# A second backward pass that lives in the first one's buffers: deferred w2 gradients, weight transposes in steps, one fixed order on the Sync queue

## The chip, the core and the metric

The kernel runs on one core of a Trainium2 chip. The core has a matmul engine (TensorE, PE in the profile, with its weight loads listed as PEld), VectorE (DVE), ScalarE (ACT), GpSimd (POOL), and SyncE (SP), whose only work here is to issue transfers. SP, ACT and POOL each keep a queue of the transfers that they issue (SPq, ACTq, POOLq in the profile); all of these are carried out by the core's 16 DMA engines. Each engine works through its own instruction list in order and waits at semaphores for the others.

The metric is the device time of one execution, in microseconds. Before the change the median of three runs is 2060.66 us (2057.24 to 2063.25).

## The reference: what is computed

A block with two branches and its whole gradient. L = 2048 positions, D = 576 channels, F = 4608 hidden units, N = 128 states; all inputs and outputs are bf16.

```python
xn = _layernorm(x)
s  = _A_ref(xn, ...)              # state-space convolution: y = conv(xn, K) + xn * Dskip
g  = _silu(_B_ref(xn, w1, w3, w2))   # gated FFN: (silu(xn @ w1) * (xn @ w3)) @ w2
out = x + s * g
# the convolution's kernel, per channel d and lag l
K = einsum("dn,dnl,dn->dl", Cc, exp(dt * A * l), dt * Bc).real
# and then the vector-Jacobian product for x and 11 parameters
_out, _vjp = jax.vjp(_f, A_u, A_A_re, ..., B_w1, B_w3, B_w2)
return (_out, *_vjp(grad_out))
```

So the kernel returns the output (out_0), the gradient of x (out_1), of the convolution's parameters (out_2 to out_9), and of w1, w3 and w2 (out_10, out_11, out_12). The change touches only the backward half.

## The kernel before, in words

The work is written in a tile language. A planner turns it into one instruction list for each engine: it places every instruction when its inputs and its buffer are ready in the planner's own reckoning of time, and among ready ones it takes the one with the earliest due time. `self.at(us)` sets the due time for what follows (L99). A tile pool has a number of buffers for each tag; a new tile waits until the oldest one of its tag has been used for the last time. A pool that is opened where another one was closed shares that memory, and its tiles wait for the users of the old ones.

The forward half and the first half of the backward (up to about 850 us) are not touched. The rest, in `backward` (L1080), has four parts:

- *The convolution's backward* (`ssm_bwd_conv`), in four quarters, beside the first groups below. It writes gK_dram and GXN_dram (the part of the gradient of the normalised x that comes from the convolution).
- *The groups* (`phase6_load` L1139, `phase6_group` L1171). F is cut into 18 groups of 256. For each, G and U are read back from HBM; ScalarE and VectorE turn them into the hidden h (tile h_n) and two factors (gg_n, gu_n). Then `ph` matmuls (L1188) multiply the output's gradient, kept transposed in goT and goTt, with w2's rows transposed (w2T); VectorE multiplies the result into gg_n and gu_n, which now are the gradients of the gate and the up branch. Three more steps follow: they are stored to GG_dram and GU_dram from the Sync queue (L1200); `phase6_grad2` (L1204) forms w2's gradient from h_n and go_o (two blocks of 32 matmuls in a group, L1215); `phase6_grad13` (L1222) forms those of w1 and w3 from xn and gg_n, gu_n (L1233, L1240, L1242). ScalarE copies each result out of PSUM into a tile gw, and GpSimd issues its store.
- *The parameter chunks* (`param_quarter`, L957), 36 of them. Each reads qT (a transposing transfer on the Sync queue, L969 through L1137), gK (two transfers on the Sync queue into a tile gz that was zeroed by GpSimd, L864 and L966) and pz (ScalarE's queue), makes 16 matmuls (L977), and keeps VectorE for 16 instructions (L986, L988, L991) that sum into S_all. After the last one `phase5_final` (L994) turns S_all into out_2 to out_8; its input loads (L82) and its buffers come after the chunks' ones.
- *The input-gradient tiles* (`phase6_inputs`, L1250), 16 of them, 128 positions each. A tile reads its rows of GG_dram and GU_dram transposed (ggc, guc; two transposing transfers on the Sync queue) and multiplies them with w1 and w3 transposed, 36 blocks of 128 hidden units each (tiles wTB_w in the profile): 144 matmuls into px (L1277). VectorE adds the convolution's part (L1280), and `ln_bwd_tile` (L1284) takes it back through the layernorm and stores out_1, in turn from the Sync and the ScalarE queue. ggc and guc have two buffers each.

w1 and w3 are transposed in two parts: blocks 0 to 11 by ten transposing transfers in one run during the groups (five for each weight, one for each 128 rows), into a pool of their own, and blocks 12 to 35 by ten more, in a pool that is opened after the groups' pools are closed, together with the pool of ggc and guc and with go_o, goT and goTt given up:

```python
                    self.nat_transpose(ggc[:], self.GG_dram[i])
                    self.nat_transpose(guc[:], self.GU_dram[i])
                    if i == 0:
                        wT = wT + [self.load_wT(wB, FA, FT)]
```

The due times in `backward(700, 36, 90, 15, 18, ...)` say: groups from 700 us on, 36 us each; chunks from 1060 us on, 15 us each; tiles from 1348 us on, 18 us each. Nothing else fixes the order in which chunks, stores and tile transfers stand on the Sync queue.

## Time and profile before

| | |
|---|---|
| median of the runs | 2060.66 us (2057.24 to 2063.25) |
| the profiled execution: its time, its span | 2069.67 us, 2067.9 us |
| mean granted PE clock | 0.952 |
| busy: PE, PEld, DVE, ACT, POOL | 1792.2, 1310.5, 1390.4, 880.4, 333.3 us |
| transfers over the span | 411.29 MB, 199 GB/s |
| px matmuls (L1277) | 2 x 1152 |
| w2-gradient matmuls (L1215) | 1152, in 36 blocks |
| w1/w3-gradient matmuls (L1233) | 2 x 1152 |
| stores of gw on POOLq | 144 of 64 KB, 36 of 144 KB, 36 of 32 KB |

The span is the time from the first to the last instruction in the record of one execution. A row of a timeline gives the start and the length in us, the engine, the line, the operation, the tile written and the tiles read, and how many instructions were merged; a bracket at its end is the engine's wait ahead of it and what ended that wait. On SPq the length of a transposing transfer is the time that it holds the Sync queue; it lands some microseconds later. Of a matmul, the length covers its passage through the array: neighbours overlap, so the distance from start to start tells what one costs. Idle time of an engine that is not the bottleneck costs nothing by itself.

### The profile page before, as it was taken

The page shows a single profiled execution, that of the slowest core. Times are in us where ns is not written, and L with a number is a line of the kernel's source. Part 1 is how long each engine was busy: PE and PEld are TensorE (multiplying, and loading weights), DVE is VectorE, ACT ScalarE, POOL GpSimd, SP SyncE. Part 2 cuts the span into 40 slices and gives each one's busy share as a digit, 9 for nine tenths or more (in the row PEclk, how much of TensorE's full clock was granted, in tenths as well). Part 3 has the DMA queues.
Part 4 walks back from the last instruction along what each step waited for, and adds up shares of the span by engine and source line. Part 5 has one row for each costly group of instructions (what it writes and reads, how often), then busy time and mean ns, then how long its engine had stood idle before and what let it go on. Part 6 is the DMA issues. An engine that isn't in the chain of part 4 may idle for free.

```text
span 2067.9 us, 40944 instructions
## 1 busy us (share of the span) xinstructions
PE 1792.2 (87%) x16465; PEld 1310.5 (63%) x16538; DVE 1390.4 (67%) x2563; ACT 880.4 (43%) x1612; POOL 333.3 (16%) x537
## 2 busy tenths in 40 slices
PE   1789999999996799799999999878998947999992
PEld 1444454455553577578878787766787835777781
DVE  7545556556885355459693878657788853777867
ACT  2867777776453011565554656434544400000000
POOL 5002222121113111112112121121221100000000
PEclk9999999999998899899999999999999978999996
DMA  3588777777658977537565474798887799999981
GB/s 80 205 309 288 265 252 262 261 242 241 202 188 179 250 187 188 159 117 230 161 207 155 144 215 146 174 185 208 206 227 173 180 209 219 216 207 209 233 152 22
DMA packets 626222, 411.29 MB, mean 199 GB/s; under 512 B 434608, under 2 KB 565808, under 8 KB 621424
## 3 DMA queue, kind: packets, MB, share of 16 engines
q1 hardware_dynamic: 566688, 273.44, 54.4%
q0 software_dynamic: 29520, 109.15, 16.1%
q10 hardware_dynamic: 29824, 26.09, 4.7%
q8 instruction: 129, 2.11, 0.4%
q14 instruction: 61, 0.50, 0.1%
HBM read 130.65 MB, written 185.65 MB: 153 GB/s over the span
## 4 chain that ended last, share of the span: by engine, by line
PE 19%; DVE 13%; DMA 9%; issue 5%; SPq 5%; ACT 4%; POOL 2%; POOLq 0%; DVEq 0%; ACTq 0%
PE px L1277 8%; SPq L1137 4%; PE pgw L1233 4%; PE ph L1188 2%; PE pgw L1215 2%; DMA gg_n<-G_dram 2%; DVE pr_q L986 2%; DMA w2T<-w2r 1%; DVE cm_t L635 1%; ACT gu_n L1163 1%; DMA out_dram<-gw 1%; DMA guc<-GU_dram 1%; POOL out_dram L1237 1%; DMA gs<-GS_dram 1%; PE et_ps L977 1%
## 5 line engine op out<-in xcount | busy, mean ns | idle before, releaser
L1277 PE MATMUL px<-wTB_w,guc 128*128 128x288 bf16 x1152 | 242.7, 291 | 24.8 <-DMA wTB_w<-in_B_w_dram 12.6
L1233 PEld LDWEIGHTS <-xn_bf 128*128 128x128 bf16 x2304 | 226.5, 98 | 50.0 <-issue 20.3
L1277 PE MATMUL px<-wTB_w,ggc 128*128 128x288 bf16 x1152 | 244.5, 291 | 15.4 <-DMA ggc<-GG_dram 8.1
L986 DVE TENSOR_TENSOR pr_q<-et_ps,pz 128x512 f32<-128x512 f32 x288 | 186.5, 680 | 73.2 <-PE et_ps L977 72.6
L1188 PE MATMUL ph<-w2T,goT 128*128 128x256 bf16 x1152 | 178.4, 281 | 26.1 <-ACT gh L1191 22.3
L752 PEld LDWEIGHTS <-xnT 128*128 128x128 bf16 x1152 | 104.6, 97 | 105.9 <-issue 19.9
L807 PE MATMUL po<-w2g,hc 128*128 128x288 bf16 x1152 | 148.5, 292 | 24.6 <-DMA w2g<-in_B_w_dram 24.6
L752 PE MATMUL pg<-wmB_w,xnT 128*128 128x512 bf16 x526 | 156.4, 382 | 5.5 <-ACT g_t L760 2.3
L1215 PE MATMUL pgw<-go_o,h_n 128*128 128x288 bf16 x1152 | 156.3, 292 | 0.0
L752 PE MATMUL pu<-wmB_w,xnT 128*128 128x512 bf16 x559 | 154.0, 380 | 0.9 <-ACT u_t L761 0.5
L1294 ACT ACTIVATE t<-gx 128x576 f32<-128x576 f32 x16 | 10.9, 683 | 330.5 <-DVE gx L1280 307.7
L807 PEld LDWEIGHTS <-hc 128*128 128x128 bf16 x1152 | 113.2, 99 | 56.3 <-issue 25.0
L1277 PEld LDWEIGHTS <-guc 128*128 128x128 bf16 x1152 | 113.9, 99 | 54.6 <-DMA guc<-GU_dram 13.1
L756 ACT ACTIVATE s_t<-pg 128x512 bf16<-128x512 f32 x144 | 86.3, 599 | 145.0 <-PE pu L754 115.0
L1233 PE MATMUL pgw<-gg_n,xn_bf 128*128 128x256 bf16 x1152 | 132.5, 276 | 14.4 <-ACT gw L1236 14.4
L1236 ACT CAST gw<-pgw 128x256 bf16<-128x256 f32 x144 | 53.6, 377 | 214.0 <-PE pgw L1233 166.3
L1188 PEld LDWEIGHTS <-goT 128*128 128x128 bf16 x1152 | 114.2, 101 | 46.3 <-issue 25.2
L1277 PEld LDWEIGHTS <-ggc 128*128 128x128 bf16 x1152 | 113.4, 99 | 46.0 <-DMA ggc<-GG_dram 8.3
L1233 PE MATMUL pgw<-gu_n,xn_bf 128*128 128x256 bf16 x1152 | 131.3, 273 | 3.9 <-ACT gw L1219 2.2
L1215 PEld LDWEIGHTS <-h_n 128*128 128x128 bf16 x1152 | 114.1, 100 | 29.2
L766 POOL DMA_DIRECT2D G_dram<-g_t x72 | 52.4, 728 | 496.7 <-ACT g_t L760 477.7
L476 ACT ACTIVATE cs_k<-et_ps 128x512 bf16<-128x512 int16 x216 | 116.1, 644 | 6.6 <-PE et_ps L475 6.5
(305 smaller groups left out, 3735.2 us busy)
## 6 DMA issues: line engine op xcount, KB each, us to landing
G_dram<-g_t POOLq DMA_DIRECT2D x72, 256.0 KB, 3.4
U_dram<-u_t POOLq DMA_DIRECT2D x72, 256.0 KB, 4.5
H_dram<-h_t SPq DMA_DIRECT2D x72, 256.0 KB, 3.5
Q_dram<-q_k SPq DMA_DIRECT2D x36, 512.0 KB, 3.2
gg_n<-G_dram POOLq DMA_DIRECT2D x18, 1024.0 KB, 5.6
h_n<-U_dram POOLq DMA_DIRECT2D x18, 1024.0 KB, 9.0
GU_dram<-gu_n SPq DMA_DIRECT2D x36, 512.0 KB, 5.2
GG_dram<-gg_n SPq DMA_DIRECT2D x36, 512.0 KB, 9.6
```

The source lines that it names most:

```text
L476: nc.scalar.activation(out=CS[:, :, o:o + 256], in_=pt[:].bitcast(I16)[:, :, 0::2], func=ACT.Sin, scale=6.283184 / 2 ** 16)
L752: nc.tensor.matmul(pt[:], lhsT=xnT[:, c, ts], rhs=wm[w][:, c, :], start=(c == 0), stop=False)
L756: nc.scalar.activation(out=s_t[:, :, q, :], in_=pgv, func=ACT.Silu)
L766: nc.gpsimd.dma_start(out=dst[fb * ng:(fb + 1) * ng, :, i0:i0 + NT, :].rearrange("g p t f -> p g (t f)"), in_=src[:].rearrange("p g t f -> ...
L807: nc.tensor.matmul(po_[:, pi_, 0:pw], lhsT=hc[:, fi, :], rhs=w2[fi][:, po:po + pw], start=(fi == 0), stop=(fi == FT - 1))
L986: nc.vector.tensor_tensor(out=pr[:], in0=Tv if s else Tv[:, ::-1], in1=pv, op=ALU.mult)
L1137: self.nc.sync.dma_start_transpose(out=dst, in_=src)
L1188: nc.tensor.matmul(ph[j][:, k, :].rearrange("p (a f) -> p a f", f=P), lhsT=lw, rhs=rh, start=(n == 0), stop=(n == nfull))
L1215: nc.tensor.matmul(pgw[pi_][:, 0:pw], lhsT=hn[:, tt, fl * P:(fl + 1) * P], rhs=go_o[:, tt, po:po + pw], start=(tt == 0), stop=(tt == LT - 1))
L1233: nc.tensor.matmul(pw_[:, 0:FG], lhsT=self.xn_bf[:, tt, c * P:(c + 1) * P], rhs=nat[:, tt, :], start=(tt == 0), stop=(tt == LT - 1))
L1236: nc.scalar.copy(out=gw[:], in_=pw_[:, 0:FG])
L1277: nc.tensor.matmul(px[pi_][:, 0:pw], lhsT=act[:, fi, :], rhs=wT[part][ai][:, f, po:po + pw], start=(fi == 0 and ai == 0), stop=(fi == FT - ...
```

## The change

Seven edits, all in the backward half:

1. The w2 gradients of the last two groups are left out of their groups and formed after the last group (four blocks of 32 matmuls).
2. The pools of w2T and of gg_n, h_n, gu_n stay open to the end. w1 and w3 transposed are now held as blocks 0 to 12 in the pool of their own, 13 and 14 in the two buffers of w2T, 15 to 21 and 22 to 28 in the buffers of gg_n and gu_n, and 29 to 35 in the two buffers of h_n.
3. Blocks 0 to 12 are read in five steps, two transfers behind the last store of each of the groups 11 to 15; the others in 40 smaller transfers.
4. The activations of a tile are one tile of both factors; they lie in the buffers of goT (even tiles) and go_o (odd tiles). Tile 0's are queued behind the last group's stores, tile 1's behind the weight transfers, those of tile i + 2 after tile i.
5. The chunks are made by a generator: 18 ahead of the tiles with due times as before, and the other 18 after the tiles, two each after tiles 0 and 1 and one after each later tile, with their Sync transfers behind the last activations that were queued. In a chunk, qT is now read ahead of gK. The final parameter arithmetic comes last. The three gz tiles are zeroed by VectorE.
6. A group's w1/w3 gradients are copied into one tile of four pieces and stored by one transfer for each of the two; the gw pools have two buffers where they had four.
7. out_1 is always stored from ScalarE's queue.

```diff
@@ ssm_bwd_params
-                self.nc.gpsimd.memset(z[:], 0.0)
+                self.nc.vector.memset(z[:], 0.0)
                 gz.append(z)
-            for g in range(4):
-                self.param_quarter(g, gz, S_all, qp, ps, T0 + TC * g * D // 64, TC)
+            yield
+            for ch in range(D // 16):
+                self.at(T0 + TC * ch)
+                self.param_chunk(ch, gz, S_all, qp, ps)
+                yield
@@ param_chunk
             gK = gz[ch % 3]
+            qT = qp.tile([P, 16, N], BF16, name="qT")
+            self.nat_transpose(qT[:], self.Q_dram[ch])
             for k in range(2):
                 nc.sync.dma_start(out=gK[64 * k:64 * k + 64, 1 - k].rearrange("p k f d t -> p (k f d t)"),
                                   in_=self.gK_dram[g, :, cc].rearrange("p k f h e -> p (k f h e)"))
-            qT = qp.tile([P, 16, N], BF16, name="qT")
-            self.nat_transpose(qT[:], self.Q_dram[ch])
@@ backward
+        FA, NC0 = 13, 18
         with ExitStack() as out:
+            wp = out.enter_context(pool(name="e_w", bufs=2))
+            inp = out.enter_context(pool(name="e_in", bufs=2))
             ffn = ExitStack()
...
-            gwp = ffn.enter_context(pool(name="e_gw", bufs=4))
+            gwp = ffn.enter_context(pool(name="e_gw", bufs=2))
...
-            self.at(T2 - 150)
-            wT = [self.load_wT(wA, 0, FA)]
             T1 = T0 + 4 * TQ
-            self.ssm_bwd_params(T1, TC, S_all, ps)
-            self.at(T1 + TC * D // 16)
-            self.phase5_final(out, fix, S_all, ps)
+            sums = self.ssm_bwd_params(T1, TC, S_all, ps)
+            for _ in range(NC0 + 1):
+                next(sums)
+            wT = []
+            for w in ("B_w1", "B_w3"):
+                wT.append([(0, FA, wA.tile([P, FA, D], BF16, name="wT" + w))])
             cur = self.phase6_load(0, T0 - TG, TG, wp, inp)
+            hs = []
             for gi in range(NG):
                 nxt = self.phase6_load(gi + 1, T0 + TG * gi, TG, wp, inp) if gi + 1 < NG else None
                 self.at(T0 + TG * gi)
-                self.phase6_group(gi, cur, elp, gwp, ps_h, ps_gw)
+                last = self.phase6_group(gi, cur, elp, gwp, ps_h, ps_gw, gi < NG - 2)
+                hs.append(cur[1])
+                c = gi - (NG - 7)
+                if 0 <= c < cfg.DT:
+                    with self.tc.issue_after(last.ins):
+                        for ai, w in enumerate(("B_w1", "B_w3")):
+                            do, dsz = cfg.dch[c]
+                            self.nat_transpose(wT[ai][0][2][:, :, do:do + dsz],
+                                               self.aps[w][do:do + dsz, 0:FA * P])
                 cur = nxt
+            acts = [self.load_acts(0, last)]
+            FB = FA + 2
+            for ai in range(2):
+                wT[ai].append(self.load_wT(wp, "w2T", ai, FA, FB))
+            for (ta, tb) in (("gg_n", "gu_n"), ("gg_n", "gu_n"), ("h_n", "h_n")):
+                for ai, tag in enumerate((ta, tb)):
+                    wT[ai].append(self.load_wT(inp, tag, ai, FB, FB + 7))
+                FB += 7
+            acts.append(self.load_acts(1, self.last_t))
+            self.at(T0 + TG * NG)
+            for gi in (NG - 2, NG - 1):
+                for fl in range(self.FG // P):
+                    self.phase6_grad2(gi, fl, hs[gi], gwp, ps_gw)
             ffn.close()
-            gctx.close()
-            self.phase6_inputs(T2, TX, FA, wT)
+            self.phase6_inputs(T2, TX, wT, acts, sums)
+            for _ in sums:
+                pass
+            self.phase5_final(out, fix, S_all, ps)
+        gctx.close()
@@ new: load_wT (five transfers for one weight), load_acts
+        t = pool.tile([P, f1 - f0, cfg.D], BF16, name=f"wT{ai}_{f0}", tag=tag)
+        w = self.aps[("B_w1", "B_w3")[ai]]
+        for (do, dsz) in cfg.dch:
+            self.last_t = self.nat_transpose(t[:, :, do:do + dsz], w[do:do + dsz, f0 * P:f1 * P])
+        return (f0, f1, t)
+
+    def load_acts(self, i, after):
+        t = self.gop.tile([P, 2, self.cfg.FT, P], BF16, name="acts", tag="go_o" if i % 2 else "goT")
+        with self.tc.issue_after(after.ins):
+            self.nat_transpose(t[:, 0], self.GG_dram[i])
+            self.last_t = self.nat_transpose(t[:, 1], self.GU_dram[i])
+        return t
@@ phase6_grad13
+            gw = gwp.tile([P, nfull, FG], BF16, name="gw13")
             for c in range(nfull):
...
-                gw = gwp.tile([P, FG], BF16, name="gw13")
-                nc.scalar.copy(out=gw[:], in_=pw_[:, 0:FG])
-                nc.gpsimd.dma_start(out=aps[oname][c * P:(c + 1) * P, fb:fb + FG], in_=gw[:])
+                nc.scalar.copy(out=gw[:, c], in_=pw_[:, 0:FG])
+            nc.gpsimd.dma_start(out=aps[oname][0:nfull * P, fb:fb + FG].rearrange("(c p) f -> p c f", p=P), in_=gw[:])
@@ phase6_inputs, at the end of each tile
                 self.ln_bwd_tile(sb, sm, gx, i, go_t)
+                if i + 2 < LT:
+                    acts.append(self.load_acts(i + 2, self.last_t))
+                with self.tc.issue_after(self.last_t.ins):
+                    for _ in range(2 if i < 2 else 1):
+                        next(sums, None)
@@ ln_bwd_tile
-        self.dma(out1[i * P:(i + 1) * P, :], o1[:])
+        nc.scalar.dma_start(out=out1[i * P:(i + 1) * P, :], in_=o1[:])
```

`issue_after(x)` queues what its block issues on x's engine behind x: an order of issue, not a wait for x to finish. `sums` is the generator of the chunks.

## The prediction

> **What bounds the kernel now.** I read the page's slices first, then the busy time of each engine by stage, then the Sync queue and the matmul engine in order of time where the stages meet, and last VectorE after the last matmul.
>
> ```profile
> PE   1789999999996799799999999878998947999992
> ...
> DMA  3588777777658977537565474798887799999981
> ```
>
> Each digit is 51.7 us. PE is at nine tenths nearly everywhere; the low slices in the second half are number 32 (about 1655 to 1706 us) and the last. DMA is full where PE is low, and stays full to the end. So PE is the bound, except at the seam between the group loop and the input-gradient tiles, and at the tail.
>
> ```profile
> 1360.00:1460.00 100.00, 82.05 (x737) 68.07 (x735) 70.01 (x117) 40.56 (x68) 19.49 (x36) 0.90 0.94 204
> ...
> 1660.00:1760.00 100.00, 58.56 (x464) 43.88 (x462) 44.95 (x80) 3.04 (x8) 2.76 (x6) 0.78 1.05 214
> ...
> 1860.00:1960.00 100.00, 99.58 (x857) 78.63 (x855) 79.81 (x146) 3.88 (x10) 0.00 (x0) 1.00 1.17 220
> ```
>
> Columns: stretch, length, busy time of PE, weight loads, VectorE, ScalarE, GpSimd, then granted clock, DMA share, GB/s. At the seam PE idles 41 us in 100, later not at all, and 18 us in 1360 to 1460.
>
> ```profile
> 1651.05 3.34 SPq L1200 DMA_DIRECT2D GG_dram<-gg_n  x2
> 1665.67 6.42 SPq L1137 DMA_TRANSPOSE ggc<-GG_dram  x1
> 1672.18 6.29 SPq L1137 DMA_TRANSPOSE qT<-Q_dram  x1
> 1678.59 4.73 SPq L1137 DMA_TRANSPOSE guc<-GU_dram  x1
> 1683.37 34.16 SPq L1137 DMA_TRANSPOSE wTB_w<-in_B_w_dram  x10
> ```
>
> This is the Sync queue at the seam: tile 0's activations go out only when the last group's last matmul (1665.6) has freed the memory, and ten weight transposes hold the queue for 34 us. Tile 1 runs from 1735.3.
>
> ```profile
> 1334.40 0.37 PE L1240 MATMUL pgw<-gg_n,xn_bf 128*64 128x256 bf16 x1 [4.31 <-ACT gw L1236]
> ...
> 1386.19 6.29 PE L1233 MATMUL pgw<-gg_n,xn_bf 128*128 128x256 bf16 x32 [8.71 <-ACT gw L1236]
> ...
> 1413.38 1.01 PE L1188 MATMUL ph<-w2T,goT 128*128 128x256 bf16 x4 [8.19 <-ACT gh L1191]
> ```
>
> The bracket is PE's wait. The first two are ScalarE waiting for a gw buffer whose store has not landed; the third goes back, in the chain, to a Sync queue full of weight transposes (1367 to 1390) that held the stores of the group.
>
> ```profile
> 2000.40 0.68 DVE L991 TENSOR_REDUCE S_all<-pr_q 128x8 f32<-128x512 f32 x1
> ...
> 2049.84 0.15 DVE L1068 CAST gl_bf<-glogdt 128x5 bf16<-128x5 f32 x1
> ```
>
> VectorE at the tail: the last parameter chunk ends at 2001.1, the final parameter arithmetic runs to 2049.84, and the store of gl_bf ends the span 18.1 us later, at 2067.9. PE is done at 2026.4, tile 13 at 1987.6.
>
> **The change, part by part.** The end is the sum of four stretches: E, the end of the last group's w1/w3 gradients; E to S1, the start of tile 1; S1 to T13, the end of tile 13; T13 to the span's end. Before: 1665.6, 69.7, 252.3, 80.3.
>
> *E.* Four w2-gradient blocks leave the groups: 32 matmuls take 3.92 us start to start (1645.19 to 1649.11), so 15.7 us go behind E. Their 8 ScalarE copies and 4 GpSimd stores go with them, beside idle engines (ScalarE 3 us busy in 100 at the seam). One gw13 tile for four copies with one store, 36 stores where there were 144, takes away most waits for a gw buffer: 1.68, 4.31, 8.71 and 1.80 us (1277 to 1470). The first 12 weight blocks, loaded in one run of ten transposes, become 13 blocks in five steps of two, queued behind the stores of groups 11 to 15, which takes the cause of the 8.19. Together 24.7; I take 20, since VectorE is 94% busy around 1500 and can take the place. The steps themselves stand ahead of the next chunk's qT on the Sync queue; that queue has gaps of 10 to 20 us in each group, and a late qT cost 5.2 us once (1564.7). I take 3, less 1.1 for one chunk fewer (18 against 19 so far). The gz memsets go from GpSimd (1.8 us each, 11 us waiting) to VectorE: between 0 and 5.3 us of VectorE, in a stretch where it is 70% busy; nothing on PE. E' = 1665.6 - 15.7 - 20 + 2 = 1632. Ends: 1625 (24.7 gained, steps free) and 1652 (no stall goes).
>
> *E to S1.* Activations 0 go into the goT buffer, free once the last ph matmuls are done, so they wait for the GG store alone: its issue ends 11 us before E, landing takes 9.6 us from issue, so they start at E - 3. A pair takes the Sync queue 12 us (1951.2 to 1963.5), landing 5 us later: E + 14. The rest of the weights: blocks 13 to 21 go into buffers of group 16 and can be out before; 22 to 28 wait for E; 29 to 35 for the deferred gradients (E + 15.7); activations 1 stand behind all of these. Ten transposes became forty: the two small ones that go alone on the queue show 1.2 us at 5 blocks (w2T) and 1.3 at 12 (the smallest of wTB_w), so I take 1.25 each where seven blocks at 34.16 / 216 = 0.158 would give 1.1. Queue: E + 9, + 12.5, + 12.5, + 12 = E + 46, landed E + 51. PE meanwhile does the 15.7 us and tile 0 (17.6 us), with a wait for blocks 29 to 35. So S1' = E' + 51 where it was 69.7. Ends: 46 (at the rate per block) and 76 (all forty behind activations 0).
>
> The Trainium skill speaks against this part: "DMA: Bandwidth & Descriptors", under "Rules for kernel authors", says to join many small transfers into one large one, and under "Anatomy of one DMA" it gives a fixed 2.0 us for each DMA on the GpSimd path. By that figure each of the twenty transposes that stand between activations 0 and 1 would take 2.0 us in place of 1.25, and the span would end 15 us later than by my sum, at 2072 and so a little behind the kernel before (an estimate from that page). No transpose of this trace shows it: the queue's row of 1.2 us is of the same kind of transfer and decides.
>
> *S1 to T13.* Thirteen tiles of 144 matmuls at 0.1225 us (17.64 us) and 15 chunks at 1.14 us of PE are 246.4; before had 6 us of waits. The order on the Sync queue is now activations i+2, then the chunk. It still is just in time: 12.1 us on the queue and 5 to land, against a tile of 18.8. Tiles 0 and 1 carry two chunks each, and the fourth qT waits for a buffer of the second: 3 us more. The out_1 store goes from the Sync to the ScalarE queue: 8 issues of 0.54 us, hidden behind the matmuls. 255; ends 247 and 265.
>
> *T13 to the end.* This is the cost. Chunks 33, 34 and 35 stand behind activations 15, which need tile 13's buffer. So chunk 33 is read from T13 + 12, its qT takes 2.3 us and gK 1.2, and landing 3.7: it can begin at T13 + 19.3. A chunk keeps VectorE for 9.5 us (four times 2.38, 1899.4 to 1908.9), so three are 28.5; the layernorm parts of tiles 14 and 15 add 4.0 each (L1280 to L1306); then the final arithmetic, 2001.1 to 2049.8 less the 4.0 of tile 14 that lay in it, 44.8; then 18.1. Sum 118.7, where it was 80.3: before, the last chunk was read at 1963.6, ahead of T13, and the arithmetic ran beside tile 15. Its buffers lie where the chunks' were, so it can't start sooner. Ends: 111 (chunk 33 at T13 + 16, tile 15's part after gl_bf) and 130 (a slower pair, as 9.1 and 8.3 us have been seen, and matmuls placed late).
>
> Sum: 1632 + 51 + 255 + 119 = 2057, against 2067.9: 11 us less. The profiled execution took 2069.67, 1.8 around its span, and was 9.0 above the median of the runs; so 2060.66 - 11 = **2050**.
>
> **Rivals.** *The transposes come late (slower).* If the Sync queue takes the forty transposes behind activations 0, S1' is E' + 76: the span ends at 2082, 14 longer. It decides from 11 us of lateness on. For it: the queue is in order, and ten held it 34 us before. Against: blocks 13 to 21 have free buffers a whole group earlier.
>
> *The group stalls stay (slower).* If transfers, not buffers, made them, E' is 1652, the end 2077. For it: DMA 0.94 in that stretch. Against: 8.71 came with the burst, which is spread now.
>
> *The tail does not grow.* If the last chunks are read in time, the end is T13' + 38.8 + 41.6 = 1938 + 80 = 2018, 50 less. For it: VectorE has 4.8 us free in each tile. Against: the queue's order is fixed by the code.
>
> *The two cancel.* The gain up to T13 (1987.6 against 1632 + 51 + 255 = 1938, 50 us) and the tail's cost of 38 lie so close that a miss of 5 us in either brings no change that can be measured; this is the middle of the cases above, and gets what they leave within 6 us.
>
> **How the numbers follow.** About 0.3% (6 us) is what a measurement of this kernel can tell from no change. Forecast 0.50, 0.08 of it within 6 us; no longer tail 0.09, faster; late transposes 0.16, 0.03 of it within; stalls that stay 0.16, 0.04 of it within; other mishaps 0.09, slower. Faster 0.51, same 0.15, slower 0.34. The ends of the four terms give 2029 to 2121 in span if all fall on one side; the low end of the range is near the rival without a longer tail, the high one past late transposes and half of the worst sum: 2022 to 2080 in time. The forecast's own range is 2035 to 2066.
>
> **What the profile after would show.** PE idle in the 70 us behind the last group under 20 us; tile 0 less than 25 us behind the last w1/w3 gradient; no PE wait over 3 us for gw; the last chunk's reductions after PE's last matmul, some 15 us, and a tail of about 80 us from PE's end in place of 41.6. Wrong if: transposes of blocks 13 to 21 stand behind activations 0, PE waits in the tiles for qT placed too early, or the final arithmetic starts beside tile 15.

## The result, and the profile after

The changed kernel takes 2154.18 us (median of four runs, 2145.76 to 2159.52) where the kernel before takes 2061.95 (2057.24 to 2067.92): a ratio of 1.0442, with a 95% interval of 1.0397 to 1.0486. It is 4.4% slower; the forecast was 2050, faster by 0.5%. The profiled execution after took 2159.52 us, its span is 2157.5, its mean PE clock 0.937.

The four stretches that the prediction adds up, in both profiles (E is the end of the last group's w1/w3 gradients, S1 the start of tile 1, counted from where PE has both factors of its activations, T13 the end of tile 13):

| stretch | before | predicted | after | after less predicted |
|---|---|---|---|---|
| start to E | 1665.6 | 1632 | 1644.9 | +12.9 |
| E to S1 | 69.7 | 51 | 48.9 | -2.1 |
| S1 to T13 | 252.3 | 255 | 354.2 | +99.2 |
| T13 to the end | 80.3 | 119 | 109.5 | -9.5 |
| span | 2067.9 | 2057 | 2157.5 | +100.5 |

So the loss lies in the thirteen tiles in the middle, in which nothing was expected to change. The slices of the page of the changed kernel (each 53.9 us) show it:

```profile
PE   2889999999997997999899999979888777777770
...
DMA  3598777766649975375754657999979977777751
```

PE is at eight and then seven tenths from slice 29 to the last but one, where it was at nine tenths nearly everywhere before, and DMA, which was nearly full there, is at seven tenths from slice 33 on. Neither is the bound any more. The same by stretches, with the columns of before (length, PE, weight loads, VectorE, ScalarE, GpSimd, granted clock, DMA share, GB/s):

```profile
1360.00:1460.00 100.00, 87.29 (x810) 72.52 (x809) 77.29 (x129) 46.21 (x74) 14.19 (x24) 0.92 0.99 221
1660.00:1760.00 100.00, 77.96 (x615) 59.29 (x612) 46.28 (x82) 3.03 (x8) 0.54 (x1) 0.90 1.00 196
1860.00:1960.00 100.00, 72.89 (x569) 56.98 (x567) 45.32 (x82) 2.33 (x6) 0.00 (x0) 0.86 0.77 149
```

The groups (first row) are better than before (82.05 us of PE), and so is the stretch that held the seam (second row, 58.56 before; E now lies 15 us ahead of it); the tiles (third row) fell from 99.58 to 72.89. The clock is 0.86 there.

What PE waits for in the tiles, from the waits between S1 and T13 (total, times, longest, in us):

```profile
PE et_ps L978 <- DMA gz<-gK_dram: 84.2, 12, 8.9
PE px L1305 <- DMA acts<-GU_dram: 5.3, 1, 5.3
```

Twelve waits in thirteen tiles, 7.0 us on average, all for gz, the last transfer of a parameter chunk. The second line is the one wait that ends at S1 itself and so belongs to E to S1. The kernel before has none for gz here; its first wait (4.2) ends at S1 too, and 3.4 us lie in the stretch:

```profile
PE px L1277 <- DMA guc<-GU_dram: 7.6, 2, 4.2
```

One tile of the changed kernel, first the Sync queue (SPq), then PE:

```profile
1771.90 4.57 SPq L1170 DMA_TRANSPOSE acts<-GG_dram  x1
1776.52 6.86 SPq L1170 DMA_TRANSPOSE acts<-GU_dram  x1
1783.47 2.85 SPq L1170 DMA_TRANSPOSE qT<-Q_dram  x1
1786.42 1.18 SPq L969 DMA_DIRECT2D gz<-gK_dram  x2
...
1798.72 6.89 SPq L1170 DMA_TRANSPOSE acts<-GG_dram  x1
```

```profile
1771.70 6.53 PE L1305 MATMUL px<-wTB_w,acts 128*128 128x288 bf16 x52
1778.07 6.17 PE L1305 MATMUL px<-wT,acts 128*128 128x288 bf16 x49
1789.97 1.44 PE L978 MATMUL et_ps<-gz,qT 128*128 128x128 bf16 x12 [5.74 <-DMA gz<-gK_dram]
1791.20 2.13 PE L1305 MATMUL px<-wT,acts 128*128 128x288 bf16 x8
1793.12 0.63 PE L978 MATMUL et_ps<-gz,qT 128*128 128x128 bf16 x4
1793.55 5.14 PE L1305 MATMUL px<-wT,acts 128*128 128x288 bf16 x35
```

The reader can follow the loop. At 1771.7 a tile ends; this frees its activation buffer, and at 1771.90 the activations for two tiles on are issued. The chunk's qT and gK stand behind them, and are issued by 1787.6; gz has landed at 1789.97, 18.1 us after the tile's end. PE has started the next tile at 1771.7 and has done 52 + 49 = 101 of its 144 px matmuls (12.4 us) when it comes to the chunk's matmuls, which its list has at this place. It waits 5.7 us, and 43 px matmuls stand behind the wait. They end at 1798.5, only then is the buffer free, and the next activations go out at 1798.72. So each tile's end waits for a chunk whose transfers could start only at the end of the tile before. The period is 26.8 us here and 27.6 on average (2048.04 less 1771.90, over ten tiles), where the prediction had a tile of 18.8.

At the tail, VectorE's last chunk and final arithmetic:

```profile
2096.23 0.68 DVE L992 TENSOR_REDUCE S_all<-pr_q 128x8 f32<-128x512 f32 x1
...
2140.30 0.16 DVE L1069 CAST gl_bf<-glogdt 128x5 bf16<-128x5 f32 x1
```

The last chunk is done 48.9 us after T13 (2048.0), the arithmetic takes 43.4 behind it, and the span ends 17.2 later: the long tail came as foreseen.

### The profile page after: what moved, and what is told of

It is laid out like the page before. It is cut to its first block, busy times and chain, and to the rows that moved or that the text cites. A ratio compares the mean times of both kernels' runs of the same rounds, so it can differ in the third digit from the quotient of the medians.

```text
span 2157.5 us, 40689 instructions
## 1 busy us (share of the span) xinstructions
PE 1811.9 (84%) x16465; PEld 1325.5 (61%) x16538; DVE 1397.4 (65%) x2566; ACT 881.0 (41%) x1612; POOL 278.9 (13%) x426
## 4 chain that ended last, share of the span: by engine, by line
PE 21%; SPq 10%; DMA 10%; DVE 9%; issue 5%; ACT 3%; POOL 1%; ACTq 0%; POOLq 0%; DVEq 0%
SPq L1170 10%; PE pgw L1269 7%; PE px L1305 5%; PE ph L1221 3%; PE pgw L1250 3%; DMA gg_n<-G_dram 2%; DMA qT<-Q_dram 2%; DMA gz<-gK_dram 2%; PE et_ps L978 2%; DVE cm_t L635 1%; DVE pr_q L987 1%; PE pgw L1275 1%; DMA w2T<-w2r 1%; ACT gu_n L1196 1%; PE et_ps L598 1%
## 5 line engine op out<-in xcount | busy, mean ns | idle before, releaser
L1305 PEld LDWEIGHTS <-acts 128*128 128x128 bf16 x2304 | 232.6, 102 | 76.3 <-DMA acts<-GU_dram 5.6
L1305 PE MATMUL px<-wT,acts 128*128 128x288 bf16 x1472 | 207.4, 302 | 4.7 <-DMA wT<-in_B_w_dram 4.7
L1221 PE MATMUL ph<-w2T,goT 128*128 128x256 bf16 x1440 | 187.5, 280 | 24.5 <-ACT gh L1224 20.0
L1221 PEld LDWEIGHTS <-goT 128*128 128x128 bf16 x1440 | 142.1, 100 | 49.0 <-issue 22.7
L1328 ACT ACTIVATE t<-gx 128x576 f32<-128x576 f32 x16 | 10.9, 682 | 380.7 <-DVE gx L1309 377.4
L978 PE MATMUL et_ps<-gz,qT 128*128 128x128 bf16 x576 | 58.6, 252 | 123.5 <-DMA gz<-gK_dram 91.5
L978 PEld LDWEIGHTS <-qT 128*128 128x128 bf16 x576 | 46.2, 114 | 137.5 <-issue 89.3
## 6 DMA issues: line engine op xcount, KB each, us to landing
GG_dram<-gg_n SPq DMA_DIRECT2D x36, 512.0 KB, 10.6
```

The source lines that it names most:

```text
L978: nc.tensor.matmul(T[h][:, :, dd].rearrange("p r k (f t) -> p r (k f) t", f=2), lhsT=qT[:, dl, :], rhs=gK[:, :, :, :, 8 * h + dl // 2, :]. ...
L1221: nc.tensor.matmul(ph[j][:, k, :].rearrange("p (a f) -> p a f", f=P), lhsT=lw, rhs=rh, start=(n == 0), stop=(n == nfull))
L1305: nc.tensor.matmul(px[pi_][:, 0:pw], lhsT=act[:, ai, fi, :], rhs=wT[ai][n][2][:, fi - f0, po:po + pw], start=(fi == 0 and ai == 0), stop=( ...
```

## The experiments

Each run's time is put beside runs of the kernel before on the same chip. Theory A was formed from the rows above: the place of the chunk's matmuls in PE's list makes the loss, through the loop. Theory B: the transfers themselves have become too slow for the tiles. Three more runs take two parts, singly and together, into the kernel before, to see what the groups' steps are worth.

**1. a1_sums_later: the chunk's matmuls behind the tile.** The chunk is split into its loads, which stay where they are on the Sync queue, and its matmuls and sums.

```diff
+                with self.tc.issue_after(pe.ins):      # pe: the tile's last px matmul
+                    self.params_sums()                 # chunks loaded after the tile before
                 if i + 2 < LT:
                     acts.append(self.load_acts(i + 2, self.last_t))
                 with self.tc.issue_after(self.last_t.ins):
-                    for _ in range(2 if i < 2 else 1):
-                        next(sums, None)
+                    self.params_load(2 if i < 2 else 1)
```

> The changed kernel with the Sync queue as it is, but on the matmul engine the 16 matmuls of a chunk no longer stand behind 101 of the 144 px matmuls of the tile after the one that queued the chunk's transfers: they are issued behind the last px matmul of that tile, so that the data have some 6 to 9 us more to land, and the last two chunks stand behind tile 15. Theory A (the place of the chunk's matmuls in a tile makes the wait; the wait holds back the tile's end, this the next activations, these the next chunk): the waits for gz of 5.7 to 8.9 us in each tile go, S1 to T13 falls from 354 to 255 us (at most 275), the end of it to span's end grows by up to 6 from 109.5; the time is 2055 to 2080. Rival B (the transfers are what is slow: activations, qT and gK one behind the other on one queue take a tile's time and more): the wait for gz goes over to a wait of the same size for the activations, S1 to T13 stays over 330, the time 2140 to 2165.

Measured: 2063.18 us (ratio to the kernel before 1.0004, 0.9971 to 1.0036; the changed kernel has 1.0442, some 90 us more). Its Sync queue:

```profile
1801.88 4.55 SPq L1187 DMA_TRANSPOSE acts<-GG_dram  x1
1806.47 5.22 SPq L1187 DMA_TRANSPOSE acts<-GU_dram  x1
1811.74 3.31 SPq L1187 DMA_TRANSPOSE qT<-Q_dram  x1
1815.09 1.70 SPq L978 DMA_DIRECT2D gz<-gK_dram  x2
1821.70 4.75 SPq L1187 DMA_TRANSPOSE acts<-GG_dram  x1
...
1840.38 4.59 SPq L1187 DMA_TRANSPOSE acts<-GG_dram  x1
```

The order and the durations are those of the changed kernel, and a tile comes every 18.7 to 19.8 us. S1 to T13 is 250.4 us (354.2 after), the waits for gz in it are 2.2. Nothing was done to a transfer, so theory B falls. Theory A's numbers came in but for the tail, which grew by 10.9 us where 6 was the most expected: with a chunk's matmuls behind the tile, the sums of four chunks (32 of 288 reductions) are left for VectorE after T13, where the changed kernel has a little over three (26). The four stretches are 1639.5, 44.6, 250.4 and 120.4: with this one order changed, the sum of the prediction (1632, 51, 255, 119) holds within 8 us in each term and within 3 in the span (2054.9 against 2057).

**2. k122_later_in_tile: a dose in between.** The edit of run 1, but the chunk's matmuls are issued behind px matmul 122 of 144 instead of behind all.

```diff
-                with self.tc.issue_after(pe.ins):
+                with self.tc.issue_after(self.mid.ins):   # the 122nd px matmul of the tile
                     self.params_sums()
```

> The changed kernel with a chunk's matmuls issued behind 122 of a tile's 144 px matmuls, where the changed kernel has them behind 101 and a1_sums_later behind all. Theory A as a sum: the period of a tile is the landing of the chunk, counted from the end of the tile before (27.4 - 1.5 - 43 x 0.135 = 20.1 us in the changed kernel), plus the chunk's matmuls (1.5) and the px matmuls left behind them (22 x 0.135 = 3.0): 24.6 us, at least 22; S1 to T13 290 to 320, time 2105 to 2140. Rival (the wait is all or nothing: what counts is only that the chunk stands inside a tile): the period stays at 27 and the time at 2145 to 2160; or it is gone, and the time is 2063.

Measured: 2112.46 us (ratio 1.0255, 1.0213 to 1.0298). S1 to T13 is 307.3, and from 1779.04 to 1997.48 nine tiles take 24.3 us each, where 24.6 was worked out; both other numbers lie in their ranges too. PE in one tile:

```profile
1872.00 6.53 PE L1322 MATMUL px<-wTB_w,acts 128*128 128x288 bf16 x52
1878.37 8.74 PE L1322 MATMUL px<-wT,acts 128*128 128x288 bf16 x70
1892.56 1.44 PE L994 MATMUL et_ps<-gz,qT 128*128 128x128 bf16 x12 [5.45 <-DMA gz<-gK_dram]
```

Behind 101, 122 and 144 px matmuls the period over the same nine tiles (the ends of tiles 4 to 13) is 27.7, 24.3 and 19.0 us. The loss is not all or nothing: while PE waits, the period is the chunk's landing plus what is left of the tile behind it.

**3. a2_free_chunks: no fixed order for the later chunks.** Only the `issue_after` around the chunks' generator goes; the planner then puts their transfers and matmuls where its due times ask for them.

```diff
-                with self.tc.issue_after(self.last_t.ins):
-                    for _ in range(2 if i < 2 else 1):
-                        next(sums, None)
+                for _ in range(2 if i < 2 else 1):
+                    next(sums, None)
```

> The changed kernel without the order of issue around the chunks that come after the tiles begin: their transfers stand where the planner puts them, their matmuls at the tiles' starts, the last ahead of tile 14. The activations keep their fixed order. Theory A: S1 to T13 is 255 us as it was 252 in the kernel before, no wait for gz over 2 us; the last chunk is done by tile 14, so T13 to the end is 80 to 90 as in the kernel before; with E' at 1645 and S1' at 1694 the span ends at 2028 to 2045. Rival B (transfers too slow for the tile): S1 to T13 over 330, time over 2100.

Measured: 2046.22 us (ratio 0.9899, 0.9848 to 0.9950). S1 to T13 is 251.3, with no wait for gz, as expected, and the tail is 75.1, some 5 us below what was expected. But E to S1 is 70.3 where 49 was expected: three reads of qT and three of gK now stand among the weight transposes of the seam (1662.45 to 1680.44), and PE has a wait of 19.8 us for a qT there. So one of the seven edits, the fixed place of the later chunks, carries the whole loss; without it the rest is a gain of 1%.

**4 to 6. The groups' steps, in the kernel before.** The sixth edit alone (one tile of four pieces and one store; two buffers):

```diff
-            gwp = ffn.enter_context(pool(name="e_gw", bufs=4))
+            gwp = ffn.enter_context(pool(name="e_gw", bufs=2))
...
+            gw = gwp.tile([P, nfull, FG], BF16, name="gw13")
...
-                nc.scalar.copy(out=gw[:], in_=pw_[:, 0:FG])
-                nc.gpsimd.dma_start(out=aps[oname][c * P:(c + 1) * P, fb:fb + FG], in_=gw[:])
+                nc.scalar.copy(out=gw[:, c], in_=pw_[:, 0:FG])
+            nc.gpsimd.dma_start(out=aps[oname][0:nfull * P, fb:fb + FG].rearrange("(c p) f -> p c f", p=P), in_=gw[:])
```

> The kernel before with the sixth edit alone: a group's w1 or w3 gradient is copied into one tile of four pieces with one store, and the gw pools have two buffers where they had four. If buffers made the waits for gw (my step: 1.68 + 4.31 + 8.71 + 1.80 = 16.5 us), the time falls by 10 to 17 us, to 2043 to 2051. Rival (the transfers were late, whatever the buffers: the DMA share is 0.94 there): within 4 us of before, the wait goes over to another tile or engine.

The third edit alone, for its first part (blocks 0 to 11 in five steps of two transfers):

```diff
-            wT = [self.load_wT(wA, 0, FA)]
+            wT = [[wA.tile([P, FA, D], BF16, name="wT" + w) for w in ("B_w1", "B_w3")]]
...
+                if 0 <= c < cfg.DT:
+                    with self.tc.issue_after(last.ins):
+                        for ai, w in enumerate(("B_w1", "B_w3")):
+                            do, dsz = cfg.dch[c]
+                            self.nat_transpose(wT[0][ai][:, :, do:do + dsz], self.aps[w][do:do + dsz, 0:FA * P])
```

> The kernel before with its blocks 0 to 11 of the transposed weights read in five steps of two transfers, behind the last stores of groups 11 to 15, instead of ten in one run. If the run on the Sync queue made the 8.19 us wait at 1413 and the 8.71 at 1386, the time falls by 8 to 17 us (2044 to 2052). Rival (the steps delay the qT of the chunk behind them by 2 to 7 us each, and PE waits for these): no gain, up to 10 us slower, with new waits of PE for qT between 1430 and 1650.

And both together:

> The kernel before with the edits of b1_gw13_merged and of b2_wT_steps together. My step had 24.7 us of PE waits in the groups that these two parts remove together (1.68, 4.31, 8.71, 1.80 and 8.19), 20 after a discount, 18 with the cost of the steps. By that the time is 15 to 24 us under the kernel before. Alone they gave 0.7 and 0.8% (14 and 16 us). Rival (each removes the same wait in another way, or new waits for qT take the place): 8 to 15 us under before, no more than either alone, with PE's waits for qT over 15 us in the groups.

Measured: ratios of 0.9930 (0.9896 to 0.9965), 0.9923 (0.9891 to 0.9954) and 0.9910 (0.9878 to 0.9943); times of 2056.93, 2048.42 and 2047.92 us. By the ratios they give 14 and 16 us alone and 19 together (by the medians 9, 18 and 18). So each does in the kernel before what its step said; together they give less than the 30 of the sum, though each of the three has an interval of some 7 us to either side; and 18 to 19 is what the prediction had put down for both (20, less 2). Part of what is missing shows in the waits of PE in the groups with both edits:

```profile
PE et_ps L977 <- DMA qT<-Q_dram: 14.3, 2, 7.8
```

The waits for qT were 5.5 us before. The waits for gw are 2.1 us in all now; they were 20.9 us before. The trace agrees with the times: E, counted from the first ph matmul, is 785.2 us against 805.5, and 790.4 and 790.5 with either part alone.

**7. d1_no_deferral: the first part undone.** The kernel of run 1 with the w2 gradients of groups 16 and 17 in their groups.

```diff
-                last = self.phase6_group(gi, cur, elp, gwp, ps_h, ps_gw, gi < NG - 2)
+                last = self.phase6_group(gi, cur, elp, gwp, ps_h, ps_gw, True)
...
-            for gi in (NG - 2, NG - 1):
-                for fl in range(self.FG // P):
-                    self.phase6_grad2(gi, fl, hs[gi], gwp, ps_gw)
```

> The kernel of a1_sums_later with the first part undone: the w2 gradients of the last two groups are formed in their groups again, none after the last group. My step says that the deferred 15.7 us of PE fill a stretch in which PE waits for the Sync queue: then E comes 15.7 us later, E to S1 stays at 45 to 50, and the time is 12 to 17 us more than a1_sums_later, 2075 to 2080. Rival (PE's work and not the queue bounds the seam): E 15.7 later, E to S1 15 less, the time unchanged within 4 us.

Measured: 2052.87 us (ratio 0.9967, 0.9946 to 0.9988), not above run 1 (1.0004). Neither expectation holds. E is not 15.7 us later but 2.1, counted from the first ph matmul (789.4 against 787.3), and E to S1 is 38.4. The waits of PE up to the seam, first in run 1, then here:

```profile
PE et_ps L994 <- DMA qT<-Q_dram: 30.5, 4, 14.0
PE ph L1238 <- ACT gh L1241: 19.0, 13, 3.1
```

```profile
PE ph L1235 <- ACT gh L1238: 27.4, 12, 10.6
PE et_ps L994 <- DMA qT<-Q_dram: 12.0, 2, 7.7
```

The 15.7 us of w2 gradients do work while PE would else wait: with them deferred the waits for qT are 18.5 us longer, 12.9 of them from 1570 us on, around the last two groups (6.6 and 14.0 in run 1, 7.7 here), and most of what the deferral takes out of the groups comes back as waiting. The longest wait for gh here (10.6 us at 1384.7) stands nearly 200 us ahead of these; no run shows where it comes from. Nor does the deferral help the seam: without it 26 of the 40 small transposes go out ahead of activations 0 and 14 behind them (19.2 us on the queue), where run 1 has 20 and 20, and tile 1 starts 4.1 us earlier, counted from the first ph matmul.

**8. e1_two_per_tile: the tail.** On run 1 (and with the edit of c1_small_behind_qT, which comes to nothing, see below) the chunks are read two and one in turn behind tiles 0 to 11, and the final arithmetic is asked for beside the last tiles.

```diff
-                    self.params_load(2 if i < 2 else 1)
+                    self.params_load((2 - i % 2) if i < 12 else 0)
...
+                if i == 12:
+                    self.pctx.close()
+                    self.phase5_final(out, fix, S_all, ps5)
```

> The kernel of c1_small_behind_qT with chunks 18 to 35 read two and one in turn behind tiles 0 to 11, and the final parameter arithmetic set beside the last tiles. In the trace of a1_sums_later the tail T13 to end was 120 us, 22 us of it after PE's last matmul of the tiles for VectorE's chunks 33 to 35 and 40 for the final arithmetic. Theory: with the last chunk done ahead of tile 14 the tail is 75 to 80 as in the kernel before, S1 to T13 is 255 to 262 (three more chunks in it), the time 2012 to 2025 if the small transposes no longer hold E, 2022 to 2035 if they do. Rival (VectorE with 1.5 chunks a tile, 9.5 us each and 4.0 for the layernorm, holds the tiles' ends): S1 to T13 275 or more, the time 2040 or more.

Measured: 2019.10 us (ratio 0.9797, 0.9766 to 0.9828): 2.0% under the kernel before and by the ratios some 133 us under the changed one. S1 to T13 is 258.0 as expected, the tail 74.0, a microsecond below its range; the time is 3 us below the 2022 expected for small transposes that still hold E, which they did (12.6 us of wait). VectorE at the tail:

```profile
1958.16 0.68 DVE L1008 TENSOR_REDUCE S_all<-pr_q 128x8 f32<-128x512 f32 x1
...
2002.32 0.16 DVE L1085 CAST gl_bf<-glogdt 128x5 bf16<-128x5 f32 x1
```

The last chunk is done 13.2 us after T13 (1945.65), where it was 48.9 in the changed kernel and 58.0 in run 1, and the final arithmetic of 44 us begins beside tile 14 and ends 16 us after PE's last matmul. So 45 of the 46 us between the tails of runs 1 and 8 are the earlier end of the last chunk. Its earlier read and the earlier request for the arithmetic were not tried apart.

f2_two_no_deferral is run 8 with the first part undone:

> The kernel of e1_two_per_tile with the first part undone (w2 gradients of the last two groups in their groups). In d1_no_deferral E did not come 15.7 us later but 2 us, since PE worked at these gradients while the last qT stood on the queue (its waits for qT were 12.0 us in all where a1_sums_later had 30.5). If that is so, the time here is not above e1_two_per_tile: 2010 to 2020. Rival (d1 was saved by its own order, the deferral is worth its 15.7 us): 2030 to 2036.

Measured: 2023.09 us (ratio 0.9798, 0.9765 to 0.9831), by the ratio the same as run 8, though 3 us above the expected time. The deferral of the w2 gradients gains nothing that can be measured in either surrounding.

**9 to 11. What bounds the seam.** In the changed kernel PE waits 12.5 us for the last qT ahead of group 17's last matmuls (1626.3), since ten small weight transposes (1606.58, 14.04 us) stand ahead of it on the Sync queue. Three runs move it:

```diff
# c1_small_behind_qT, on run 1: blocks 13 to 35 behind chunk 17's gK
+        with self.tc.issue_after(self.last_k.ins):
+            for (do, dsz) in cfg.dch:
                 self.last_t = self.nat_transpose(t[:, :, do:do + dsz], w[do:do + dsz, f0 * P:f1 * P])
# f1_last_qT_first, on run 8: behind chunk 17's qT
-        with self.tc.issue_after(self.last_k.ins):
+        with self.tc.issue_after(self.last_q.ins):
# g1_ten_behind_qT, on f1: blocks 13 and 14 free again
+        with (ExitStack() if f0 == 13 else self.tc.issue_after(self.last_q.ins)):
```

> The kernel of a1_sums_later with one more edit: the small weight transposes (blocks 13 to 35) stand on the Sync queue behind the transfers of chunk 17, where ten of them (14 us) stood ahead of that chunk's qT. Theory A2 (PE's wait of 12.5 to 14.0 us for qT ahead of the last group's matmuls is that queueing): the wait is under 3 us, E comes 10 to 13 us earlier counted from the first ph matmul (787 becomes 774 to 777), E to S1 stays at 45 to 50, the time is 2050 to 2054 against 2063. Rival (the seam is bound by the Sync queue's work, not by E): the same wait goes, but S1 does not move, E to S1 grows to 57 or more, the time stays at 2060 to 2066.

Measured: 2055.66 us (ratio 0.9982, 0.9954 to 1.0010). The edit missed its aim: gK of chunk 17 stands ahead of its own qT on the queue (gz has three buffers, qT two), the qT still stood behind ten transposes, and the wait was 12.4 us again. The run says nothing for or against either theory; it is in effect run 1 a second time, 0.2% from it by the ratios.

> The kernel of e1_two_per_tile with its small weight transposes (blocks 13 to 35) behind the last qT on the Sync queue. The edit of c1_small_behind_qT named the gK transfer of chunk 17, which stands ahead of its own qT, so the qT still stood behind ten transposes and PE waited 12.4 us for it. Theory A2: now this wait is under 3 us, E is 10 to 12 us earlier (789.8 us from the first ph matmul becomes 778 to 780), E to S1 stays at 47, the time falls from 2019 to 2007 to 2011. Rival (the Sync queue's work bounds the seam): the wait goes, E to S1 grows by as much, the time stays at 2016 to 2022.

Measured: 2036.88 us (ratio 0.9851, 0.9818 to 0.9884), 0.5% slower than run 8, which neither theory had. The wait was gone (E 782.3 us from the first ph matmul, against 789.8), but five transposes that had gone out a group earlier now stood behind the qT too:

```profile
1600.82 1.34 SPq L1185 DMA_TRANSPOSE qT<-Q_dram  x1
1602.20 27.70 SPq L1185 DMA_TRANSPOSE wT<-in_B_w_dram  x20
1630.01 1.32 SPq L1248 DMA_DIRECT2D GU_dram<-gu_n  x2
1631.45 3.97 SPq L1248 DMA_DIRECT2D GG_dram<-gg_n  x2
1635.52 11.64 SPq L1185 DMA_TRANSPOSE acts<-GU_dram  x1
```

The last group's stores stand behind the twenty, and the activations behind the stores: tile 1 started 845.0 us after the first ph matmul, where it was 837.2.

> As f1_last_qT_first, but the five small transposes of the first w2T buffer stay where e1_two_per_tile has them, a group earlier; only the fifteen later ones stand behind the last qT. The Sync queue then has the same work behind group 16's stores as in e1_two_per_tile, in another order. Theory Q (the seam is bound by the queue's work): PE's wait of 12.6 us for the last qT goes, E is 8 to 12 us earlier counted from the first ph matmul (789.8 becomes 778 to 782), tile 1 still starts 834 to 841 us after it (837.2 in e1_two_per_tile), E to S1 grows to 55 to 60, the time is 2015 to 2023. Rival (E bounds the seam, f1_last_qT_first lost by its five later transposes alone): tile 1 starts 825 to 829 us after the first ph matmul, time 2006 to 2012.

Measured: 2031.09 us (ratio 0.9841, 0.9813 to 0.9870). In the trace theory Q holds, to within 0.3 us of its ranges: E is 777.7 us from the first ph matmul, 12.1 earlier, and tile 1 starts at 836.4, so E to S1 has grown from 47.4 to 58.7. Of the 12.1 us that E gained, all but 0.8 were lost again before tile 1. The seam is bound by the Sync queue:

```profile
1602.40 20.26 SPq L1185 DMA_TRANSPOSE wT<-in_B_w_dram  x15
1623.08 1.00 SPq L1248 DMA_DIRECT2D GU_dram<-gu_n  x2
1624.20 4.24 SPq L1248 DMA_DIRECT2D GG_dram<-gg_n  x2
1628.53 9.91 SPq L1185 DMA_TRANSPOSE acts<-GU_dram  x1
1638.53 6.21 SPq L1185 DMA_TRANSPOSE acts<-GG_dram  x1
1644.85 28.88 SPq L1185 DMA_TRANSPOSE wT<-in_B_w_dram  x20
1673.77 5.86 SPq L1185 DMA_TRANSPOSE acts<-GG_dram  x1
```

From 1602 to tile 1 the queue has no gap over 0.5 us. The time, however, is 12 us above run 8 by the medians (9 by the ratios), outside both expectations, and 8.7 us of it lie in S1 to T13 (266.7 against 258.0), where the order of the chunks among PE's matmuls is the same in both. A pair of activations that held the queue for 17.3 us there, and a wait for gz of 5.0 behind it, account for part; why this comes in f1 (263.2) and here and not in run 8 stays open.

## Why the prediction was wrong

*The step that failed* is S1 to T13, 255 us where 354.2 came. The prediction put it so: "The order on the Sync queue is now activations i+2, then the chunk. It still is just in time: 12.1 us on the queue and 5 to land, against a tile of 18.8." This is right for the activations, and run 1 keeps that order with 250.4. What was left out is the second item: the chunk's own transfers have landed only 18.1 us after the tile's end, and its matmuls stand 12.4 us into the next tile in PE's list. The number was at hand: the prediction's own paragraph on the tail has a chunk begin "at T13 + 19.3" by the same queue, and 19.3 less 12.4 is a wait of 6.9 us in each tile; 7.0 came on average. The case was named ("PE waits in the tiles for qT placed too early") and priced with the "3 us" of one qT and an upper end of 265, because a wait was taken as a thing that happens once. It happens in every tile, because the tile's end releases the next activations and these the next chunk. The sum closes with PE's busy time in the stretch (second column), here and in run 1:

```profile
1693.80:2048.00 354.20, 269.97 (x2112) 210.60 (x2113) 187.67 (x336) 9.31 (x24) 0.00 (x0) 0.87 0.76 151
1684.10:1934.50 250.40, 246.76 (x2094) 194.27 (x2094) 181.61 (x325) 9.32 (x24) 0.00 (x0) 0.99 1.01 215
```

The 270.0 us of work and the 84.2 of waits for gz are the 354.2. Of the 103.8 us over run 1, 80.6 are waits (84.2 against 3.6), about 1 is one chunk more in the stretch, and some 22 are matmuls that ran slower behind the waits (0.87 of the clock against 0.99; see the end).

*E*: predicted 1632, measured 1644.9. In unchanged code, between 600 and 700 us, PE was busy for 72.5 us in the profile before and for 83.7 in the profile after, and the first ph matmul came 7.3 us earlier after; no run shows why. Without this luck E would have been 20 late. "I take 20" for the group stalls was right by itself: the waits for gw fell from 20.9 us to 1.6, and runs 4 to 6 gave 18 to 19 us. The term that was mis-sized is the late qT, "I take 3": PE's waits for qT rose from 5.5 to 32.1 us.

```profile
PE et_ps L978 <- DMA qT<-Q_dram: 32.1, 4, 12.5
PE ph L1221 <- ACT gh L1224: 20.0, 13, 3.0
```

14.3 us of them are there with the two steps alone (run 6), and 18.5 go with the deferral (run 7). So the 15.7 us that "go behind E" were next to no gain (2.1 us of E in run 7): they had been the cover of such waits. Right was what the profile was to show of this part: no wait over 3 us for gw (the longest is 0.6).

*E to S1*: 48.9 where 51 was predicted, and the rival of the late transposes did not come: twenty of the forty went out ahead of activations 0. That the number came out within 2.1 us is in part luck: activations 0 went out 11.3 us ahead of E (1633.64) where the prediction had 3, since the half from GU went first; against this the pair held the queue for 15.1 us in place of 12, and the twenty transposes between activations 0 and 1 for 29.9 in place of 25. The reckoning went by the queue, and g1 shows that this is the right engine to reckon by.

*T13 to the end*: 109.5 where 119 was predicted, 120.4 in run 1. Right in kind. The prediction's terms up to the arithmetic are 55.8 us (19.3, 28.5 and 8), where 48.9 came: tile 15's layernorm part lies behind the last chunk here, since tile 15 ends 48.0 us after T13. The arithmetic and the last store took 43.4 and 17.2 where 44.8 and 18.1 were taken. In run 1 the last chunk is done 58.0 us after T13, behind the sums of four chunks. Of the rivals, "The tail does not grow" did not come by itself; run 8 shows that it could be had. "The group stalls stay" was wrong in its cause, but right in that E gained little.

Three slips in the prediction's arithmetic change nothing: the low slice of 1655 to 1706 us is the thirty-third; the low end of E to S1 comes to 48 by the rate per block, not 46; and the high ends of the four terms add to 2123, not 2121.

## What to carry to other kernels

Where the order is written out by hand, follow every item through both lists: when can its transfer be issued (what stands ahead of it on its queue, and what releases that), and at which place of the consuming engine's list does its first user stand. If the release of the queue's head comes from the end of the very work that waits for the queue's tail, a lateness of a few microseconds is paid in every round. And before work is moved out of a stretch, look whether it is what keeps the engine busy there while a transfer is on its way.

## What the runs showed of the hardware that was not expected

A wait of PE costs more than its length. In the changed kernel the twelve et_ps matmuls behind a wait of 5.74 us took 1.23 us start to start (1789.97 to 1791.20), and the eight px matmuls behind them 1.92; in run 1, without a wait, the same take 0.67 and 1.10:

```profile
1840.35 0.83 PE L994 MATMUL et_ps<-gz,qT 128*128 128x128 bf16 x12
1841.02 1.14 PE L1322 MATMUL px<-wTB_w,acts 128*128 128x288 bf16 x8
1842.12 0.40 PE L994 MATMUL et_ps<-gz,qT 128*128 128x128 bf16 x4
```

That is 1.4 us lost in these rows. The granted clock ahead of the wait, behind it, and from 1795 us on (the column before the last two):

```profile
1780.00:1784.00 4.00, 4.00 (x35) 3.14 (x33) 0.00 (x0) 0.00 (x0) 0.00 (x0) 1.00 0.85 192
1790.00:1794.90 4.90, 4.90 (x30) 3.76 (x31) 4.30 (x8) 0.00 (x0) 0.00 (x0) 0.50 0.00 0
1795.00:1798.50 3.50, 3.50 (x30) 2.81 (x29) 3.50 (x7) 0.00 (x0) 0.00 (x0) 1.00 0.00 0
```

So here the half clock lasted for 5.0 us of work, and in S1 to T13 the slower matmuls come to some 22 us over run 1, about 1.8 for each of the twelve waits. The Trainium skill has the rule for this in "TensorE: Matmul & The Clock Gate", under "What's actually happening": after an idle window of about 3.4 us the array runs at half rate, until about 3.4 us of work have gone by. All twelve waits (5.4 to 8.9 us) are longer than that, and each was followed by a half clock, which lasted for 2.7 to 5.7 us of work. Shorter waits went both ways: in run 2 the matmuls behind a wait of 2.88 us (1868.28) ran at a clock of 1.00, in g1 those from 1771.0 on, behind one of 2.44 us (1770.25), at 0.50.

A transposing transfer of two or seven blocks holds the Sync queue for 1.30 us as a median of forty (1.17 to 2.59), runs of twenty for 27.7 to 29.9 us, so 1.4 to 1.5 for each. The prediction had 1.25. The Trainium skill's 2.0 us for each DMA on the GpSimd path ("DMA: Bandwidth & Descriptors", "Anatomy of one DMA"), which the prediction set against this, is for another path, and the median and the runs of twenty on the Sync queue lie below it; the row decided rightly.

Not tried by themselves are the second, the fourth and the seventh edit (the pools kept open with their small transposes, the activations in one tile in the buffers of goT and go_o, and out_1 on ScalarE's queue) and, of the fifth, qT ahead of gK with the memsets on VectorE. Runs 1 and 8 have them all and lose nothing that would point to them.
